# Squared-ReLU attention with a mixture of adapters: zero matmuls on PE at the start, another path for the first keys, and a new order of operations

## The chip, the cores and the metric

The kernel runs on one core of a Trainium2 chip. Its engines are PE (matrix multiplication), DVE and ACT (elementwise work, both can read the accumulators in PSUM), POOL (here it issues loads and builds two constant tiles) and SP (here it issues stores). Each engine works through its own instructions in the order in which they stand in the program, and waits on semaphores for the others. The metric is the time on the device in microseconds (us), the median of several runs; lower is better.

## The reference

Eight batches of twelve heads, with 448 positions and a head size of 64, go through an attention without softmax. The rows of its output, 768 wide, then go through eight adapters of rank 16, of which each row uses two:

```
scores = scale * np.matmul(q, k.transpose(0, 1, 3, 2))
attn = np.maximum(scores, 0.0) ** 2 / S
attn_out = np.matmul(attn, v)
...
logits = x @ w_gate                       # x: 3584 x 768
topk = np.argpartition(-logits, K, axis=1)[:, :K]     # K = 2
w = softmax over the two chosen logits
z = x[mask] @ A[e]                        # for each expert e of the row
delta[mask] += w[mask, k, None] * (z @ B[e])
return x + delta
```

Inputs and output are float32.

## The kernel before

**Tiling.** Four heads of one batch make a quad; there are 8 x 3 = 24 quads. A quad is cut into J = 7 pieces of PH = 64 keys. One piece of one quad is a step n, and there are 168 steps.

**A quad's and a step's work.** A quad's q, k and v are loaded by POOL (`load`, line 265: two DMAs for each tensor, which cast float32 to bfloat16 on the way). `tp` (line 376) transposes q and k on PE with an identity matrix (28 small transposes each, line 386), and DVE copies the result from PSUM into `qT` (line 400). Then each step has:

- `qk` (line 434): four matmuls of 64x64 by 64x448 that give scores (line 445)
- `relu` (line 456): one pass over 128x896 scores on ACT (line 465) or DVE (line 467)
- `sq` (line 475): squares for 2 or 3 steps at once, on DVE (line 483)
- `pv` (line 490): four matmuls with v (line 500), some six steps behind `qk`

After the seven steps of a quad, `xt_copy` (line 518) takes the sum from PSUM into `xt` in two copies on either ACT or DVE (line 529).

**Adapters.** 28 tiles of 128 rows. `gate` (line 538), for up to three tiles at once: logits and low-rank products on PE (line 546), a chain of small operations on DVE and ACT that picks two experts and gives their weights (lines 567 to 590), and a transpose (line 607) which is copied to `zT` (line 616). `outputs` (line 623), for one tile in two halves: the sum of x and the adapters on PE (lines 634 and 639), a copy to `osb` on ACT or DVE (line 656), and stores issued by SP (line 666). `aw_place` (line 330) brings A and w_gate into the order of the rows by matmuls with a selection matrix `sel`.

**What sets the order.** `build` (line 228) lists all operations with durations, dependences, buffers and a rank. `schedule` (line 88) is a planner that runs when the program is built: it plays the operations through with assumed durations and, on each engine, takes the available one of lowest rank (for PE with a few rules on top). The result is a fixed order for each engine and, for operations that may go to ACT or DVE, a fixed engine. Nothing of it is decided on the chip.

**The start.** `first` (line 278) treats the first quad's keys separately. The first CUT = 3 pieces come uncast by the hardware queues of SP and ACT into `raw` (line 283), and DVE casts them to `k_first` (line 298). The other four pieces come through POOL with a cast, as `k_rest` (line 294). ACT runs a warm-up activation (line 287) which loads its function table. POOL builds the identity (line 290). In `tp` the first quad has copies of its own (line 408): keys of `k_first`, queries in two halves on DVE and ACT, keys of `k_rest`. Then POOL loads in the order q1, k1, v0, q2, k2, v1, and so on (line 683 on): the v of a quad follows the q and k of the quad after it.

Of the kernel before, what the change touches and what calls it, by code (L numbers as in the profile page):

```python
# [13 lines left out]

J = 7
CUT = 3
PH = 64
QUADS = 3
NB = 8
# [7 lines left out]
PARTS = {b: ((0, S),) for b in range(NB)}  # L27

def parts(*cuts):
    x = [0, *cuts, S]
    return tuple(zip(x, x[1:]))
# [2 lines left out]
C = dict(  # L36
    tp_=2.3287, qk_=-3.679, sq_=3.7975, pv_=3.3372, xt_=-1.2131, gate_=-0.65203, id_=-0.78412,
    out_=-0.80943, zt_=6.6019, a12=(4, 7), late=6, merge_x=0, id2=2.6063, ocap=3, sqs=(2, 2, 3),
    slack=0.12309, switch=3.3127, third=4.3408, dve_relu=0.55845, relu_until=400, qk=-2.3217, sq=10,
    pv=1.0506, xt=8.4423, tp=-9.2867, tpe=4.3867, gate_mm=-4.8593, gate=-1.4524, zt=0.2432, zte=2.902,  # L40
    id=15.183, out=3.032, pace=6.5353,
)
POOLS = dict(qT=5, a1=C["a12"][0], a2=C["a12"][1], zp=2, zT=3, osb=6, w=3, q=4, k=4, v=6)

MODE_SWITCH = 0.13
HOP = 0.05
RAW = {"PE": 0.0, "ACT": 0.2, "DVE": 0.115, "POOL": 0.0, "SP": 0.0}
LAT = {"PE": 0.18, "ACT": 0.19, "DVE": 0.084, "POOL": 0.0, "SP": 0.0}
# [28 lines left out]
class Dma:  # L77


    def __init__(self, rate=0.4):  # L80
        self.rate, self.free = rate, 0.0

    def land(self, t, mb):
        self.free = max(self.free, t + 0.5) + mb / self.rate
        return self.free + 1.4


def schedule(ops, c=C):

    free = {e: 0.0 for o in ops for e in o.engs}
    avail = {e: [] for e in free}
    level = dict(POOLS, lane=4)
    freed = {b: 0.0 for b in range(c.get("nb", 8))}
    used = {"s": 0, "t": 0, "p": 0, "m": 0, "y": 0, "o": 0}
    cap = {"s": 3, "t": 1, "p": 2, "m": 2, "y": 1, "o": c.get("ocap", 1)}
    events, returns = [0.0], []
    dma = Dma()
    mode = None  # L100
    relus = []
# [13 lines left out]
    def choose(o):  # L115
        k, n = o.want
        if used[k] >= cap[k]:
            return None
        slots = sorted((x for x in range(0, c.get("nb", 8), 2) if x in freed and x + 1 in freed),
                       key=lambda x: max(freed[x], freed[x + 1]))  # L120
        if k == "s":
            if used["s"] >= 2 and any(
                x.want and x.kind != "qk" and x.ready <= t + 1e-9 and x.rank <= o.rank + c["third"]
                for x in avail["PE"]
            ):
                return None
            return [slots[0], slots[0] + 1] if slots else None
        halves = sorted((x for x in freed if x ^ 1 not in freed), key=lambda x: freed[x])
        if n == 1 and halves:
            return halves[:1]  # L130
        busy = c.get("nb", 8) // 2 - len(slots) - used["s"]
        if not slots or busy >= c.get("nb", 8) // 2 - 2:
            return None
        if n == 1 and busy == 1 and any(
            x.want and x.ready <= t + 1e-9 and x.kind in ("pv", "tp") and x.rank <= o.rank
            for x in avail["PE"]
        ):
            return None
        return [slots[0], slots[0] + 1][:n]
# [19 lines left out]
    while left:  # L159
# [9 lines left out]
        for e in free:  # L169
            if free[e] > t + 1e-9:  # L170
                continue
            o = pick(e)
            if o is None:
                continue
            st = t
            if e == "PE":
                if mode is not None and o.mode != mode:
                    st = max(t, free[e] + MODE_SWITCH)
                mode = o.mode
            o.start, o.eng = st, e  # L180
            free[e] = st + o.dur[e]
            if o.kind == "load":
                o.end = dma.land(free[e], o.mb) + (o.lat or 0.0)
            else:
                o.end = free[e] + (LAT[e] if o.lat is None else o.lat)
            for x in o.engs:
                avail[x].remove(o)
            for p in o.take:
                level[p] -= 1
            if o.want is not None:  # L190
                o.banks = choose(o)
                for x in o.banks:
                    del freed[x]
                used[o.want[0]] += 1
            back = o.end + HOP
            for p in o.give:
                returns.append((back, p))
            for owner, i in o.free:
                k = owner.want[0]
                if i is None:  # L200
                    returns.append((back, "bank", owner.banks, k, 1))
                else:
                    returns.append((back, "bank", [owner.banks[i]], k, 1 / len(owner.banks)))
            events.append(back)
            for u in o.users:
                u.missing -= 1
                near = u.engs == (e,) and o.kind != "load"
                u.ready = max(u.ready, st if u.after is o else free[e] + RAW[e] if near else back)
                if not u.missing:
                    for x in u.engs:  # L210
                        avail[x].append(u)
                    events.append(u.ready)
                    if u.kind == "relu":
                        relus.append(u)
            if o.kind == "relu":
                relus.remove(o)
            events.append(free[e])
            order.append(o)
            left -= 1
            moved = True  # L220
# [7 lines left out]
def build(k=None, c=C):  # L228
# [49 lines left out]
    def first():  # L278

        def dma(eng, g):
            eng.dma_start(out=k.raw[g * PH : g * PH + PH], in_=k.qkv[1][0, g, :, 0:2, : CUT * PH])

        def warm():
            nc.vector.memset(k.warm, 0.0)
            nc.scalar.activation(k.warm, k.warm, ACTF.Sigmoid)

        def ident():
            make_identity(nc, k.identf)  # L290

        def rest():
            for g in range(2):
                nc.gpsimd.dma_start(out=k.k_rest[g * PH : g * PH + PH],
                                    in_=k.qkv[1][0, g, :, 0:2, CUT * PH :])

        def cast():
            nc.vector.tensor_copy(k.k_first, k.raw)

        ds = [op(("SP",), 0.8, lambda: dma(nc.sync, 0), kind="load", rank=-50.0),  # L300
              op(("ACT",), 0.8, lambda: dma(nc.scalar, 1), kind="load", rank=-50.0)]
        for d in ds:
            d.mb = 2 * CUT * PH * 64 * 4e-6
        op(ACT, 1.4, warm, rank=-49.0)
        q0 = load(0, 0, 0, [])
        oi = op(("POOL",), 0.6, ident)
        ob = op(DVE, 0.2, lambda: nc.vector.tensor_copy(k.identb, k.identf), deps=[oi], rank=-60.0)
        k0 = op(DVE, dve(2 * CUT * PH, 1.92), cast, deps=ds + [ob], rank=-50.0)
        k1 = op(("POOL",), 1.17, rest, kind="load", take=("lane",), give=("lane",))
        k1.mb = 4 * (S - CUT * PH) * 64 * 4e-6  # L310
        return q0, k0, k1


# [309 lines left out]
    def outputs(tl):  # L623
# [3 lines left out]
        v = due[tl]  # L627
        W = 64 * DO
        evs, obs, prev = [], {}, None
        for h in range(2):  # L630

            def f_b(h=h):
                for x in range(3):
                    nc.tensor.matmul(  # L634
                        out=bank(obs[h])[:, x * 128 : x * 128 + 128],
                        lhsT=k.xt[:, 3 * h + x, c0 : c0 + 128], rhs=k.identb,
                        start=(x == 0), stop=False, skip_group_check=True,
                    )
                nc.tensor.matmul(  # L639
                    out=bank(obs[h])[:, :W], lhsT=T["zT", g0][:, zi], rhs=k.B[:, h * W : h * W + W],  # L640
                    start=False, stop=True, skip_group_check=True,
                )

            last = False
            if h:
                zuse[g0] -= 1
                last = zuse[g0] == 0
            prev = op(PE, 0.81, f_b, mode="128", kind="b", deps=[o_zT, b_load] + xdeps[tl], after=prev,
                      banks=("o", 1), take=() if h else ("osb",), give=("zT",) if last else (),
                      rank=v + at("id", v) + (c["id2"] if h else 0), ni=10)  # L650
            obs[h] = prev

            def ev(cp, h=h):
                if ("osb", tl) not in T:
                    new("osb", ("osb", tl), [128, 128 * DO], F32)
                cp(T["osb", tl][:, h * W : h * W + W], bank(obs[h])[:, :W])  # L656

            evs.append(evac(W, ev, deps=[prev], free=[(prev, 0)], rank=v + at("out", v)))

        def st():  # L660
            r = 0
# [18 lines left out]
        if (b, w, q) not in loaded:  # L680
            loaded[b, w, q] = load(b, w, q, [])

    for i in range(len(tiles_of) + 1):
        if i < len(tiles_of):
            loads(i, 0)
            loads(i, 1)
        if i:
            loads(i - 1, 2)
        if i == 2:
            sel_op = op(("POOL",), 1.5, sel_fn)  # L690
            a_load = op(("POOL",), 1.5, aw_fn, kind="load")
            a_load.mb = 0.4
# [4 lines left out]

    groups, t = [], 0
    while t < NT:
        m = min(3, NT - t)  # L700
        if NT - t == 4:
            m = 2
        if t == NT - 2:
# [41 lines left out]
            finish(n - c["late"] - 1)  # L745
    for n in range(NS - c["late"] - 1, NS):
        finish(n)
    return ops


@with_exitstack
def kernel(
# [31 lines left out]
    h.a_raw = const.tile([128, E, DO, R], BF16)  # L784
    h.g_raw = const.tile([128, DO, E], BF16)
    h.raw = const.tile([128, 2, CUT * PH], F32)
    h.k_first = const.tile([128, 2, CUT * PH], BF16)
    h.k_rest = const.tile([128, 2, (J - CUT) * PH], BF16)
    h.warm = const.tile([1, 8], F32)
# [39 lines left out]
```

## Time and profile before

| | us |
|---|---|
| median of 8 runs | 186.65 |
| lowest and highest | 185.52 and 187.75 |
| the profiled execution | 186.15 |
| its span, first to last instruction | 184.4 |

Busy time over the whole span, from the profile:

| engine | busy us | share |
|---|---|---|
| PE, matmuls | 168.5 | 91% |
| ACT | 161.1 | 87% |
| DVE | 159.0 | 86% |
| PE, weight loads | 99.5 | 54% |
| POOL | 90.3 | 49% |

The largest groups of instructions in it:

| line, engine, what | count | mean ns |
|---|---|---|
| 465 ACT, relu 128x896 | 162 | 952 |
| 483 DVE, squares of two steps | 48 | 1082 |
| 483 DVE, squares of three steps | 24 | 1575 |
| 529 DVE, xt copy | 42 | 618 |
| 656 ACT, output copy | 45 | 495 |
| 639 PE, half of an output | 112 | 514 |

The means of ACT and DVE include the start and end of an instruction, which overlap with its neighbours: in a row, one follows another sooner than that. Matmuls of 64x64 weights run four at a time in different parts of the array. A line of idle time such as "[0.93 <-PE ps L445]" says how long an engine stood still before the instruction and which instruction, by engine, tile and line, released it. Idle time counts only on an engine that sets the end, so the stages have to be looked at one by one.

### The profile page before, as it was taken

The numbers are of one execution on the slowest core, as the hardware profiler recorded it, in microseconds if no ns is written. First come the engines' busy times: TensorE is split into PE (matmuls) and PEld (weight loads), VectorE is DVE, ScalarE is ACT, GpSimd is POOL, SyncE is SP. The second block draws the span as 40 slices with busy tenths as digits, with TensorE's granted clock in tenths as the row PEclk, the third lists the DMA queues.
The fourth block names the chain that finished last, engine by engine and source line by source line (L and its number), as shares of the span: only waits on it lengthen the run. The fifth ranks groups of instructions, "written<-read, shape, count | busy, mean of one in ns | idle before, by whom it ended". The sixth has DMA issues, their size and how long they took to land.

```text
span 184.4 us, 7480 instructions
## 1 busy us (share of the span) xinstructions
PE 168.5 (91%) x3236; PEld 99.5 (54%) x3236; DVE 159.0 (86%) x249; ACT 161.1 (87%) x234; POOL 90.3 (49%) x155
## 2 busy tenths in 40 slices
PE   0779988889999999989999999999999999999990
PEld 0435865545555645664566455656565556556640
DVE  1499999999999999999999999999999999853600
ACT  3597899999999999999999999999999999954350
POOL 7999889898964927375735754571100000000000
PEclk9999999999999999999999999999999999999997
DMA  4999999999999999799999999999430333344775
GB/s 91 129 169 167 189 168 182 190 173 179 185 210 238 210 197 193 102 191 167 164 184 169 167 175 191 127 191 232 81 88 1 89 89 91 85 108 111 211 196 147
DMA packets 26801, 28.71 MB, mean 156 GB/s; under 512 B 4432, under 2 KB 23120, under 8 KB 26768
## 3 DMA queue, kind: packets, MB, share of 16 engines
q0 software_dynamic: 22000, 17.03, 65.9%
q1 hardware_dynamic: 4624, 11.11, 20.6%
q8 instruction: 25, 0.41, 0.9%
q10 hardware_dynamic: 144, 0.10, 0.2%
q14 instruction: 8, 0.07, 0.1%
HBM read 33.84 MB, written 11.01 MB: 243 GB/s over the span
## 4 chain that ended last, share of the span: by engine, by line
PE 56%; DVE 18%; ACT 12%; issue 5%; POOL 4%; DMA 3%; ACTq 0%; POOLq 0%
PE ps L639 17%; PE ps L445 12%; PE ps L500 12%; ACT a L465 11%; DVE a L483 9%; PE ps L634 6%; PE ps L546 4%; DVE xt L529 3%; PE ps L386 3%; DVE qT L400 3%; DMA q<-in_q_dram 3%; POOL q L271 1%; PE ps L607 1%; DVE zp L590 1%; POOL k L271 1%
## 5 line engine op out<-in xcount | busy, mean ns | idle before, releaser
L465 ACT ACTIVATE a<-ps 128x896 bf16<-128x896 f32 x162 | 139.0, 952 | 4.0 <-PE ps L445 3.7
L483 DVE TENSOR_TENSOR a<-a 128x1792 bf16<-128x1792 bf16 (+1 forms) x72 | 88.3, 1246 | 0.4 <-ACT a L465 0.4
L445 PE MATMUL ps<-qT 64*64 64x448 bf16 x672 | 62.0, 378 | 3.9 <-ACT a L465 2.3
L639 PE MATMUL ps<-B,zT 128*128 128x384 f32 x112 | 48.4, 514 | 0.0
L500 PE MATMUL ps<-a,v 64*64 64x448 bf16 x672 | 44.6, 360 | 0.7 <-DVE qT L400 0.5
L271 POOL DMA_DIRECT2D v<-in_v_dram x48 | 29.1, 623 | 28.6 <-PE ps L386 13.0
L445 PEld LDWEIGHTS <-qT 64*64 64x64 bf16 x672 | 23.6, 108 | 33.9 <-issue 24.8
L271 POOL DMA_DIRECT2D q<-in_q_dram x48 | 29.2, 627 | 6.6 <-PE ps L386 2.6
L271 POOL DMA_DIRECT2D k<-in_k_dram x46 | 28.1, 633 | 3.7 <-PE ps L445 2.4
L500 PEld LDWEIGHTS <-v 64*64 64x64 bf16 x672 | 22.6, 109 | 12.6 <-issue 4.9
L656 ACT COPY osb<-ps 128x384 f32<-128x384 f32 x45 | 22.3, 495 | 7.0 <-PE ps L639 5.9
L529 DVE CAST xt<-ps 128x448 bf16<-128x448 f32 x42 | 24.9, 618 | 3.8 <-PE ps L500 3.5
L400 DVE COPY qT<-ps 128x1792 bf16<-128x1792 bf16 x23 | 24.9, 1082 | 0.9 <-PE ps L386 0.6
L634 PE MATMUL ps<-identb,xt 128*128 128x128 bf16 x168 | 18.8, 221 | 0.1
L634 PEld LDWEIGHTS <-xt 128*128 128x128 bf16 x168 | 11.3, 97 | 13.2 <-issue 11.5
L639 PEld LDWEIGHTS ps<-B,zT 128*128 128x128 f32 x112 | 16.9, 191 | 0.0
L386 PEld LDWEIGHTS <-q 64*64 64x64 bf16 x672 | 10.9, 114 | 4.6 <-DMA q<-in_q_dram 2.0
L546 PE MATMUL ps<-awg,xt 128*128 128x136 bf16 x168 | 13.4, 224 | 0.0
L546 PEld LDWEIGHTS <-xt 128*128 128x128 bf16 x168 | 10.1, 98 | 4.8 <-issue 4.3
L386 PE MATMUL ps<-identb,q 64*64 64x64 bf16 x672 | 11.2, 199 | 0.8 <-DMA q<-in_q_dram 0.6
L386 PE MATMUL ps<-identb,k 64*64 64x64 bf16 x644 | 11.0, 199 | 0.5 <-issue 0.5
L386 PEld LDWEIGHTS <-k 64*64 64x64 bf16 x644 | 9.3, 109 | 1.7 <-DMA k<-in_k_dram 0.9
(41 smaller groups left out, 71.5 us busy)
## 6 DMA issues: line engine op xcount, KB each, us to landing
out_dram<-osb SPq DMA_DIRECT2D x56, 192.0 KB, 3.1
q<-in_q_dram POOLq DMA_DIRECT2D x48, 112.0 KB, 4.4
v<-in_v_dram POOLq DMA_DIRECT2D x48, 112.0 KB, 4.4
k<-in_k_dram POOLq DMA_DIRECT2D x46, 112.0 KB, 4.8
B<-in_moe_B_dram POOLq DMA_DIRECT2D x1, 384.0 KB, 5.3
a_raw<-in_moe_A_dram POOLq DMA_DIRECT2D x1, 192.0 KB, 4.1
k_rest<-in_k_dram POOLq DMA_DIRECT2D x2, 64.0 KB, 3.2
raw<-in_k_dram SPq DMA_DIRECT2D x1, 96.0 KB, 3.5
```

The costliest lines, as they stand in the source:

```text
L271: nc.gpsimd.dma_start(out=t[g * PH : g * PH + PH], in_=k.qkv[w][b, g, :, 2 * q : 2 * q + 2, :])
L386: nc.tensor.transpose(k.ps_b[sl * PH : sl * PH + PH, o.banks[g], (w * J + j) * PH : (w * J + j) * PH + PH], source(w, j)[r, sl], k.identb[ ...
L400: nc.vector.tensor_copy(t.rearrange("p g w x -> p g (w x)"), k.ps_b[:, m.banks[0] : m.banks[0] + 2, : 2 * S])
L445: nc.tensor.matmul(out=bank(o, sl)[g * PH : g * PH + PH, at : at + w], lhsT=t[r, g, 1, j * PH : j * PH + PH], rhs=t[r, g, 0, x0:x1], start ...
L465: nc.scalar.activation(out, flat(qk_ops[n], w), ACTF.Relu, scale=k.relu_scale)
L483: nc.vector.tensor_mul(a2, T["a1", g0], T["a1", g0])
L500: nc.tensor.matmul(out=bank(head, g)[sl * PH : sl * PH + PH, :w], lhsT=vn[r, sl, j * PH : j * PH + PH], rhs=T["a2", g0][r, i, sl * w : sl ...
L529: evac(w, lambda cp, g=g: cp(k.xt[:, g * QUADS + q, b * S + x0 : b * S + x1], bank(src, g)[:, :w]), deps=[pv_ops[n]], free=[(src, g)], ran ...
L546: nc.tensor.matmul(out=bank(zops[0])[:, t * ZW : t * ZW + ZW], lhsT=k.xt[:, do, 128 * tiles[t] : 128 * tiles[t] + 128], rhs=k.awg[:, do, : ...
L634: nc.tensor.matmul(out=bank(obs[h])[:, x * 128 : x * 128 + 128], lhsT=k.xt[:, 3 * h + x, c0 : c0 + 128], rhs=k.identb, start=(x == 0), sto ...
L639: nc.tensor.matmul(out=bank(obs[h])[:, :W], lhsT=T["zT", g0][:, zi], rhs=k.B[:, h * W : h * W + W], start=False, stop=True, skip_group_che ...
L656: cp(T["osb", tl][:, h * W : h * W + W], bank(obs[h])[:, :W])
```

## The change

Five things are edited.

1. **Zeros on PE.** A tile `zeros` is cleared by DVE, and PE multiplies it by itself SPIN = 8 times, 128x128 by 128x512, into PSUM bank 7, before the first transposes. Nothing reads the result.
2. **k_rest.** It now comes uncast by ACT's queue into `raw_rest`, in two DMAs that stand right behind that of `raw`, and DVE casts it.
3. **v one quad later.** The list of loads puts the v of a quad behind the q and k of the quad two further on.
4. **The planner's assumptions.** Engines begin at given times, PE takes twice as long until COLD = 7.0 us, and loads land by other formulas; four constants of `C` change.
5. **Ranks and engines.** RANKS shifts the ranks of some 150 operations by number, loads among them, and ENGINES fixes 16 operations to ACT or DVE.

New options (`bfull`, `merge_o`, `keep`, `gsz`) have defaults that leave the program as it was.

```diff
+SPIN = 8
...
-    slack=0.12309, switch=3.3127, third=4.3408, dve_relu=0.55845, relu_until=400, qk=-2.3217, sq=10,
+    slack=0.12338, switch=4.388, third=4.5832, dve_relu=0.20452, relu_until=400, qk=-2.3217, sq=10,
...
+RANKS = {
+    4: 25, 6: -266, 21: 137, 24: 219, 25: 204, 27: 194, 28: 242, 29: 496, 30: 237, 31: 550, 33: 638, 34:
...
+ENGINES = {
+    110: "ACT", 168: "ACT", 212: "DVE", 224: "DVE", 332: "DVE", 377: "ACT", 387: "ACT", 444: "DVE", 446:
...
+BEGIN = {"PE": 1.1, "ACT": 0.74, "DVE": 0.8, "POOL": 1.24, "SP": 0.74}
+COLD = 7.0
...
-            free[e] = st + o.dur[e]
+            free[e] = st + o.dur[e] * (2 if e == "PE" and st < COLD else 1)
...
-        def dma(eng, g):
-            eng.dma_start(out=k.raw[g * PH : g * PH + PH], in_=k.qkv[1][0, g, :, 0:2, : CUT * PH])
+        def dma(eng, t, g, j0, j1):
+            eng.dma_start(out=t[g * PH : g * PH + PH], in_=k.qkv[1][0, g, :, 0:2, j0 * PH : j1 * PH])
 
         def warm():
+            nc.scalar.activation(k.warm, k.warm, ACTF.Sigmoid)
+
+        def zeros():
             nc.vector.memset(k.warm, 0.0)
-            nc.scalar.activation(k.warm, k.warm, ACTF.Sigmoid)
+            nc.vector.memset(k.zeros, 0.0)
+
+        def spin():
+            for _ in range(SPIN):
+                nc.tensor.matmul(k.ps[:, 7, :], lhsT=k.zeros[:, :128], rhs=k.zeros, start=True, stop=True)
...
         def rest():
             for g in range(2):
-                nc.gpsimd.dma_start(out=k.k_rest[g * PH : g * PH + PH],
-                                    in_=k.qkv[1][0, g, :, 0:2, CUT * PH :])
...
+                dma(nc.scalar, k.raw_rest, g, CUT, J)
+
+        oz = op(DVE, 0.35, zeros, rank=-70.0)
+        op(PE, 0.214 * SPIN, spin, mode="128", deps=[oz], kind="spin", ni=2 * SPIN, rank=-70.0)
...
-        k1 = op(("POOL",), 1.17, rest, kind="load", take=("lane",), give=("lane",))
-        k1.mb = 4 * (S - CUT * PH) * 64 * 4e-6
+        k1 = op(DVE, dve(2 * (J - CUT) * PH, 1.92), lambda: nc.vector.tensor_copy(k.k_rest, k.raw_rest),
+                deps=[kr], rank=-30.0)
...
-    for i in range(len(tiles_of) + 1):
+    for i in range(len(tiles_of) + 2):
         if i < len(tiles_of):
             loads(i, 0)
             loads(i, 1)
-        if i:
-            loads(i - 1, 2)
-        if i == 2:
+        if i > 1:
+            loads(i - 2, 2)
+        if i == 4:
...
+    for i, d in RANKS.items():
+        ops[i].rank += d / 4
+    for i, e in ENGINES.items():
+        ops[i].engs = (e,)
```

What the planner makes of it: the work is the same but for the zeros and the cast of k_rest. Of the 168 relus DVE takes 10 (6 before), of the 48 xt copies ACT takes 21 (6 before), and of the 56 output copies DVE takes 28 (11 before). On POOL the loads begin q0, q1, k1, q2, k2, v0 (before: q0, k_rest, q1, k1, v0, q2, k2), and later loads stand in a changed order too; that of B comes seven loads later than w_gate's. On PE the transposes of k_rest stand before the first score step (before: behind it); on DVE the cast of k_rest stands before the copy of the first queries, and DVE takes the very first relu. Behind the last score step stand 17 half outputs and the gates of 7 tiles (before: 18 and 4).

## The prediction

> **What bounds the kernel now.** I read the slices first, because averages hide stages here.
>
> ```profile
> PE   0779988889999999989999999999999999999990
> ...
> DVE  1499999999999999999999999999999999853600
> ACT  3597899999999999999999999999999999954350
> ...
> PEclk9999999999999999999999999999999999999997
> ```
>
> One slice is 4.6 us. There are three stages: a ramp to about 40 us, in which ACT and DVE still stand idle at times; a plateau in which all three engines are full; and a tail from about 160 us in which only PE is. The busy time of each engine by stage gives the sizes (columns: PE, PEld, DVE, ACT, POOL, clock, DMA share, GB/s):
>
> ```profile
> 4.75:9.35 4.60, 3.75 (x104) 2.20 (x105) 2.18 (x5) 2.59 (x4) 4.60 (x9) 1.00 1.06 133
> 9.35:40.00 30.65, 26.82 (x647) 16.93 (x642) 29.45 (x39) 27.73 (x35) 28.59 (x47) 1.00 1.19 178
> ...
> 40.00:160.00 120.00, 118.51 (x2344) 68.47 (x2344) 117.68 (x176) 119.36 (x174) 53.49 (x91) 1.00 0.86 153
> 160.00:182.50 22.50, 19.37 (x149) 11.91 (x146) 9.05 (x30) 9.92 (x24) 0.00 (x0) 1.00 0.66 171
> ```
>
> On the plateau ACT is idle for 0.6 us of 120 and DVE for 2.3: **the two evacuating engines are the bound**, as most copies out of PSUM can go to either. So a microsecond that one of them loses in the ramp costs half a microsecond of span, and one that both lose costs a whole one. The tail is PE working off outputs: in the chain of waits one half output is 0.17 + 0.70 = 0.87 us.
>
> Then the timeline of the ramp shows which waits cost (start, length, engine, group, idle before it and its releaser):
>
> ```profile
> 4.34 0.36 DVE L298 CAST k_first<-raw 128x384 bf16<-128x384 f32 x1 [0.94 <-DMA raw<-in_k_dram]
> ...
> 6.04 0.39 DVE L408 COPY qT<-ps 128x448 bf16<-128x448 bf16 x1 [0.51 <-PE ps L386]
> ...
> 7.30 4.99 ACT L465 ACTIVATE a<-ps 128x896 bf16<-128x896 f32 x6 [0.68 <-PE ps L445]
> 7.52 0.42 DVE L408 COPY qT<-ps 128x512 bf16<-128x512 bf16 x1 [1.09 <-PE ps L386]
> ...
> 8.34 1.09 DVE L467 TENSOR_SCALAR a<-ps 128x896 bf16<-128x896 f32 x1 [0.39 <-PE ps L445]
> ...
> 17.92 2.74 ACT L465 ACTIVATE a<-ps 128x896 bf16<-128x896 f32 x3 [0.93 <-PE ps L445]
> ```
>
> ACT's waits after 7.30 us are 0.21 (at 12.49), 0.23 (14.45) and 0.93 (17.92), then 0.64, 0.32, 0.30 and 0.17 up to 40 us, all for scores. DVE's from 9.35 us are 0.27, 0.35, 0.32 and 0.26.
>
> Last, the groups of matmuls by shape, in the windows 8 to 18 us and 20 to 40 us:
>
> ```profile
> L445 PE MATMUL ps<-qT 64*64 64x448 bf16 x44 | 5.8, 569 | 0.8 <-DVE qT L400 0.8
> L500 PE MATMUL ps<-a,v 64*64 64x448 bf16 x25 | 3.0, 574 | 0.0
> ```
>
> ```profile
> L445 PE MATMUL ps<-qT 64*64 64x448 bf16 x88 | 9.0, 361 | 1.9 <-ACT a L465 1.6 <-issue 0.2
> L500 PE MATMUL ps<-a,v 64*64 64x448 bf16 x84 | 6.0, 352 | 0.2 <-DVE awg L345 0.2
> ```
>
> The same matmul takes 570 ns before about 18.4 us and 355 after. In the chain, 18 matmuls of weights times v fill 1.93 us at 15.56, and 20 fill 0.95 later: **half rate**. The clock row reads 9 throughout, so only the durations show it.
>
> **The change, part by part.**
>
> *Zeros on PE.* DVE's new memset follows one at 0.80 us, so PE starts at about 1.25. Half rate is about 0.38 us per four-matmul step of 448 columns (1.93 x 4/18 = 0.43 with drain), so a full-array matmul of 512 columns is about 0.43 us by estimate, and eight end at 1.25 + 3.4 = 4.7, just where k_first is cast (4.70). They delay the first transposes by 0 to 0.3 us; I take 0.1.
>
> Does it speed the clock up? The row: PE was almost gapless from 6.49 to 11.04 us (4.5 us, gaps of about 0.1) and stayed slow; it sped up at 18.4 after a gapless stretch from 13.4. By that row, 3.4 us of zeros and a few transposes do nothing. The rule is in the Trainium skill, "TensorE: Matmul & The Clock Gate", section "What's actually happening": the clock is released after a busy window of about 3.4 us, and the windows run free of the kernel's start. By it, 18.4 was a window's end, the one before ended at 15.0, and 8.2 to 11.6 failed through the 0.81 us gap at 11.04, so the trace agrees. The rule also speaks against the change: zeros exactly as long as one window seldom fill one. But if they miss, the next stretch can serve, and the clock would be up by about 10 us. By the rule ACT's waits of 0.21, 0.23 and 0.93 (1.37 us), which fall where score and value steps run at half rate, mostly go; by the row alone, none do. I take the rule, and **1.1 us of ACT**.
>
> *k_rest by ACT's queue, uncast.* POOL loses two issues of 0.61 us. ACT gains two of 0.72, so its table load moves from 1.50 to about 2.94 and its warm-up ends near 4.45; its first work is at 6.09, so 1.6 us of cover is left. DVE gains a cast of about 0.43 (the 128x512 copy took 0.42). It now stands ahead of the copy of the first queries; behind it on DVE wait that copy, the copy of the other keys and the first relu, and all score steps wait for the query copy. PE, too, transposes k_rest ahead of the first score step. By the landing times of raw (2.7 and 3.5 us from issue) the two pieces, issued at 1.46 and 2.2, land between 4.2 and 5.7; cast by 6.1 at the latest, so the copy at 6.04 slips by 0 to 0.1.
>
> Against it stands a rule, in "DMA: Bandwidth & Descriptors", "Issuing engines are not separate DMA queues": all queues share the 16 DMA engines, so another queue saves issue time only. The rows agree that the engines are full (share 1.06 from 4.75 us). Over the first 20 us SP's 96 KB took 2.3% of the engines, 0.46 us; so k_rest's 256 KB in float32 is about 1.1 us of all engines, now ahead of or among the first queries (landed by 5.46). By the issue rows the slip is 0, by the rule up to 1.1. I take 0.3, nearer the issue rows because the engines moved nothing before 2.2 us, and keep 1.1 for the range.
>
> *Order of loads.* q1 and k1 issue one slot (1.17 us) earlier, but the same bytes lie ahead of them, so I count nothing. Third queries and keys pass the first v: 13.39, the end of the longest DMA piece in the chain (5.00 us), comes about 1.2 earlier; that feeds the waits already counted. First v issues near 7.8 instead of 6.60 and lands, at 4.8 us, by 12.6; it is needed at 15.42. Later, some loads of q and k are created only 7 or 8 score steps ahead of use (30 before); at 0.9 to 1.0 us per step that covers issue and landing (1.2 + 4.4) by about 1 us. Cost nothing, 1 us for each if that is gone.
>
> *Order of operations.* DVE takes the first relu. Its waits of 1.09 and 0.39 shrink, as all keys are there early: that relu starts at about 7.0 instead of 8.34, **1.3 us of DVE**. ACT starts with the second score step, at 7.3 plus the slips above (0.1 + 0.3), less 0.2 to 0.4 if the clock is up: no change. Of ACT's 1.43 us of later waits and DVE's 1.2, I take **0.4 and 0.6** as gone, about two fifths; the ends are 0 and 2.6, since a new order may close or open waits. Work moved, by step in back-to-back runs: 4 relus to DVE, 4 x (1.01 - 0.83) = +0.7; 15 xt copies to ACT, 15 x (0.41 - 0.53) = -1.8; 7 output copies to DVE ahead of the tail, 7 x (0.48 - 0.36) = +0.8. Together -0.3, counted as nothing.
>
> *Tail.* After the last score step 17 half outputs are left instead of 18 (-0.87), but gates of 7 tiles instead of 4 (3 x 0.39 = +1.2). +0.3, set against the 0.15 of the moved work: nothing.
>
> **Sum:** (1.1 + 1.3 + 0.4 + 0.6)/2 = 1.7 us. From the profiled execution's 186.15 (span 184.4) that gives 184.45; the median of the runs is 0.5 above that execution, so for the median **184.9 us**.
>
> **Rivals.** *The shared DMA engines decide (20%), slower.* k_rest holds up the first queries by 1.1 us, its cast adds 0.4 ahead of their copy, and PE's gap after the zeros is then so long that the clock stays down. Both engines lose 1.5; only 0.4 + 0.6, halved, comes back: 186.65 + 1.5 - 0.5 = 187.65. It decides once the first relu starts after 7.8. For it: the full engines. Against: POOL's k_rest already overlapped the queries' landing.
>
> *The clock doesn't turn, and the new order replaces old waits by equal ones (20%).* Only the early relu counts: 186.65 - 0.65 = 186.0. For it: the 4.5 us stretch without effect.
>
> *The order closes nearly every wait (8%).* Ramp 1.37 + 1.43 + 1.3 + 1.2 and half of the plateau's 2.9 idle, halved: 3.4, so 183.2. Against: an order fixed beforehand meets durations that vary.
>
> **Numbers.** Forecast 52%. Runs of this kernel spread so that 0.5% (0.93 us) is about the least that can be told from no change. Faster: nearly all of the forecast, the best case and a little of the second rival, 0.60; same 0.22; slower 0.18. Range: down to all ramp and plateau waits gone, 8.2/2 = 4.1, so 182.5; up to the first rival, 187.6.
>
> **What would show it.** Matmuls of 64x448 near 355 ns before 11 us (570 up to 18 refutes the zeros); first DVE relu near 7.0 and first ACT relu by 7.4 (7.8 or later means the DMA rival); ACT's wait near 18 us gone; DVE's and ACT's idle from 9.35 to 40 us down by 2; plateau idle unchanged; the last score step 1.7 us earlier than 159.3 and the tail as long as before. More than 1.5 us of new waits for q or k after 40 us would make the forecast wrong.

## The result and the profile after

The changed kernel is slower: a median of 191.21 us (187.90 to 194.96, 20 runs) against 186.80 for the kernel before on the same chip (185.52 to 188.27, 55 runs). The ratio is **1.015, with an interval of 1.012 to 1.019**; it compares only executions within 1.5% of the fastest of their kernel, which are 6 of the 20 after and all 55 before, and so lies below the quotient of the medians, 1.024. The forecast was 184.9, with a range up to 187.6.

The profile read here is of an execution of 188.04 us with a span of 186.3. Its slices (4.66 us each):

```profile
PE   7657986789999999799699999999999999999990
...
DVE  1699997999999999999699999999999999987660
ACT  3499997999999999799699999999999999931100
```

The plateau has holes that it did not have before. In the slices at 74.5 and 88.5 us PE and ACT fall to 7 and 6, in the second of them DVE too; another hole stands at 28 us. The busy time by stage gives their size (columns: stage and its length, then PE, PEld, DVE, ACT, POOL, clock, DMA share, GB/s). First the kernel before, then the changed one:

```profile
40.00:100.00 60.00, 58.81 (x1188) 33.35 (x1188) 58.93 (x85) 59.88 (x87) 38.03 (x65) 1.00 1.07 183
```

```profile
9.35:40.00 30.65, 23.85 (x705) 15.18 (x700) 29.18 (x36) 29.29 (x40) 28.24 (x48) 1.00 1.21 180
40.00:100.00 60.00, 55.45 (x1098) 31.07 (x1097) 56.65 (x85) 56.86 (x80) 35.25 (x61) 1.00 1.01 173
```

From 40 to 100 us ACT does 3.0 us less of work and DVE 2.3 us less: (3.0 + 2.3)/2 = 2.65 us of span, by estimate. From 100 to 160 next to nothing changes (DVE 59.2 against 58.8, ACT 59.4 against 59.5). In the ramp the two engines do more than before (29.18 + 29.29 against 29.45 + 27.73), so that a part of the expected gain is there: 1.3 us of the two. The last score step starts at 161.05 us instead of 159.32, and from there to the end it is 25.2 us as against 25.1: the tail is as long as before.

PE's timeline says what the plateau waits for:

```profile
49.84 0.41 PE L422 MATMUL ps<-identb,k 64*64 64x64 bf16 x26 [0.36 <-DMA k<-in_k_dram]
...
76.48 0.22 PE L422 MATMUL ps<-identb,q 64*64 64x64 bf16 x2 [0.38 <-DMA q<-in_q_dram]
...
77.31 0.41 PE L422 MATMUL ps<-identb,q 64*64 64x64 bf16 x26 [0.62 <-DMA q<-in_q_dram]
...
90.07 0.22 PE L422 MATMUL ps<-identb,q 64*64 64x64 bf16 x2 [0.91 <-DMA q<-in_q_dram]
...
91.00 0.41 PE L422 MATMUL ps<-identb,q 64*64 64x64 bf16 x26 [0.71 <-DMA q<-in_q_dram]
```

Three loads come late: one k and two q, 2.98 us of PE in all. Before, PE's timeline shows no wait for a load between 40 and 100 us. How late they are differs from one execution to the next: in the profile of another one, of 194.46 us, PE waits 6.30 us in that stretch, for the same three. A transpose that waits holds up all of PE, which works in order; then the scores are late, and ACT, full until then, stands still (1.67 us before its relu at 91.92), and so does DVE (1.59 us before its copy at 91.76).

POOL's timeline says why the loads are late; its columns are start and length of the issues, and x6 means three loads of two DMAs:

```profile
41.30 3.56 POOL L300 DMA_DIRECT2D v<-in_v_dram  x6
44.84 1.22 POOL L300 DMA_DIRECT2D k<-in_k_dram  x2
...
68.95 1.19 POOL L300 DMA_DIRECT2D v<-in_v_dram  x2 [2.91 <-PE ps L481]
70.12 1.22 POOL L300 DMA_DIRECT2D k<-in_k_dram  x2
71.28 1.24 POOL L300 DMA_DIRECT2D q<-in_q_dram  x2
...
82.78 1.19 POOL L300 DMA_DIRECT2D v<-in_v_dram  x2 [2.14 <-PE ps L481]
83.94 1.22 POOL L300 DMA_DIRECT2D k<-in_k_dram  x2
85.11 1.24 POOL L300 DMA_DIRECT2D q<-in_q_dram  x2
```

The program's order gives their names (the number is the quad). k8, which PE wants at 49.5, stands behind v8, v18 and v6. q12 stands behind v10, which waits 2.91 us for a buffer, and k15. q14 stands behind v23, which waits 2.14 us, and k17. Steps run in order, seven to a quad, so v18 and v23 are needed more than 80 score steps later. RANKS did that: from q1 on the loads are operations 11 to 83 of the list, and the largest shifts in RANKS are theirs. A larger shift means later; v18, operation 72, has 1134 where its neighbours 71 and 73 have 2257 and 2361, and so comes far ahead of them. (The trace names a matmul of PE as what v10 and v23 waited for. That it was a free buffer is shown below, by a run with more of them.)

### The profile page after: what moved, and what is told of

Same layout as the page of the kernel before. It is cut to its first block, busy times and chain, and to the rows that moved or that the text cites. A ratio compares the mean times of both kernels' runs of the same rounds, so it can differ in the third digit from the quotient of the medians.

```text
span 192.7 us, 7488 instructions
## 1 busy us (share of the span) xinstructions
PE 170.1 (88%) x3244; PEld 98.1 (51%) x3244; DVE 166.2 (86%) x258; ACT 156.3 (81%) x227; POOL 89.6 (47%) x153
## 4 chain that ended last, share of the span: by engine, by line
PE 38%; ACT 21%; DMA 19%; POOL 12%; issue 7%; DVE 1%; ACTq 0%; POOLq 0%
ACT a L501 17%; PE ps L676 14%; DMA k<-in_k_dram 11%; PE ps L481 8%; PE ps L536 6%; DMA q<-in_q_dram 6%; PE ps L671 4%; POOL q L300 4%; POOL k L300 3%; POOL v L300 3%; PE ps L582 3%; DMA a_raw<-in_moe_A_dram 3%; PE ps L422 2%; ACT osb L708 2%; ACT xt L565 1%
## 5 line engine op out<-in xcount | busy, mean ns | idle before, releaser
L501 ACT ACTIVATE a<-ps 128x896 bf16<-128x896 f32 x158 | 135.9, 958 | 11.3 <-PE ps L481 10.5
L481 PE MATMUL ps<-qT 64*64 64x448 bf16 x672 | 60.0, 375 | 4.7 <-ACT a L501 3.3
L676 PE MATMUL ps<-B,zT 128*128 128x384 f32 x112 | 49.1, 521 | 0.0
L536 PE MATMUL ps<-a,v 64*64 64x448 bf16 x672 | 42.6, 350 | 0.7 <-ACT a L501 0.7
L481 PEld LDWEIGHTS <-qT 64*64 64x64 bf16 x672 | 22.7, 107 | 33.8 <-issue 27.7
L536 PEld LDWEIGHTS <-v 64*64 64x64 bf16 x672 | 21.2, 106 | 10.8 <-issue 3.0
L708 DVE COPY osb<-ps 128x384 f32<-128x384 f32 x28 | 15.5, 555 | 4.5 <-PE ps L676 2.9
L565 DVE CAST xt<-ps 128x448 bf16<-128x448 f32 x27 | 16.3, 617 | 0.3
L708 ACT COPY osb<-ps 128x384 f32<-128x384 f32 x28 | 14.4, 523 | 2.2 <-PE ps L676 2.1
L422 PEld LDWEIGHTS <-q 64*64 64x64 bf16 x672 | 9.7, 110 | 10.0 <-DMA q<-in_q_dram 5.8
L422 PE MATMUL ps<-identb,k 64*64 64x64 bf16 x644 | 10.8, 198 | 3.9 <-DMA k<-in_k_dram 3.8
```

Of the source, the lines that this page charges most:

```text
L422: nc.tensor.transpose(k.ps_b[sl * PH : sl * PH + PH, o.banks[g], (w * J + j) * PH : (w * J + j) * PH + PH], source(w, j)[r, sl], k.identb[ ...
L481: nc.tensor.matmul(out=bank(o, sl)[g * PH : g * PH + PH, at : at + w], lhsT=t[r, g, 1, j * PH : j * PH + PH], rhs=t[r, g, 0, x0:x1], start ...
L501: nc.scalar.activation(out, flat(qk_ops[n], w), ACTF.Relu, scale=k.relu_scale)
L536: nc.tensor.matmul(out=bank(head, g)[sl * PH : sl * PH + PH, :w], lhsT=vn[r, sl, j * PH : j * PH + PH], rhs=T["a2", g0][r, i, sl * w : sl ...
L565: evac(w, lambda cp, g=g: cp(k.xt[:, g * QUADS + q, b * S + x0 : b * S + x1], bank(src, g)[:, :w]), deps=[pv_ops[n]], free=[(src, g)], ran ...
L676: nc.tensor.matmul(out=out(h)[:, :W], lhsT=T["zT", g0][:, zi], rhs=k.B[:, h * W : h * W + W], start=False, stop=True, skip_group_check=True,)
```

## The experiments

Three theories were open. **Order of loads**: the new sequence on POOL costs all of the loss, and without it the change would do about what was forecast. **The start**: zeros and the keys by ACT's queue cost it (the first rival). **Order of compute**: the new order of all other operations costs it, without a wait for a transfer. Several runs share one edit: after the planner is done, the loads are put into another sequence, and all other operations keep their order, on every engine.

```diff
-    for o in schedule(build(h)):
+    order = schedule(build(h))
+    loads = [o for o in order if getattr(o, "key", None)]
+    loads.sort(key=lambda o: o.seq)
+    for o in reload(order, loads):
```

`reload` goes through the order and issues the next load of the wanted sequence where a load stood, as soon as its pool has a buffer free. Sorted by `seq` that is the order of the list: q0 q1 k1 q2 k2 v0 q3 k3 v1, and so on.

**The changed kernel again, and with its loads in turn.**

> The changed kernel unedited, for a profile beside the others and its spread. All theories: 188 to 195 us. Late loads (A): PE again waits some microseconds in all for q and k between 40 and 100 us, and how long differs from run to run. Late start (B): the loss is there by 20 us. Order of compute (C): the loss is spread over the plateau without any wait on a transfer.

> The changed kernel with POOL's loads of q, k and v put back in the order in which quads need them (v one quad later, as the diff's loop has it); the order on PE, DVE, ACT and SP is untouched. A (late loads): the waits for q and k after 40 us go, and with them all of the loss: 184.5 to 186 us, ratio about 0.99. B (start): a half microsecond comes back at most, ratio still 1.01 or more. C (order of compute): the same, ratio 1.01 or more.

Again: 189.82 us (4 runs), 1.013 (1.005 to 1.022). In turn: **184.63 (4 runs), 0.989 (0.983 to 0.995)**; on another chip, with 6 runs, 184.09 and 0.983 (0.979 to 0.988). These ten runs lie within 2.5 us of each other, the 24 of the changed kernel within 7.1.

> The same program as after_loads_in_turn, beside the one without zeros on the same chip: ratio 0.987 to 0.991. If zeros help, it is at least 0.2% below the one without; if they hurt, as in the kernel before, 0.2 to 0.5% above.

The order of loads is thus worth more than the whole loss, and with the start and the order of compute as they were nothing of it is left. A stage of the run in turn (columns as above):

```profile
40.00:100.00 60.00, 58.33 (x1201) 33.58 (x1201) 59.52 (x89) 59.69 (x85) 36.59 (x63) 1.00 1.05 177
```

ACT and DVE are full again from 40 to 100 us, PE waits for no load there, and the last score step starts at 156.82, 4.2 us earlier than in the changed kernel.

**The sequence alone, put into the kernel before.** The same tool gives the kernel before the changed kernel's sequence, and nothing else of the change.

```diff
+    order = schedule(build(h))
...
+    want = "q0 q1 k1 q2 k2 v0 q3 k3 v1 q4 k4 k5 k7 v2 v3 q5 v4 ... v8 v18 v6 k8 ... v10 k15 q12 ... v23 k17 q14 ..."
+    loads.sort(key=lambda o: want.index(o.key[0] + str(o.key[1])))
```

> The converse: the kernel before with the sequence of loads of the changed kernel on POOL, everything else as before. A: slower by what the changed kernel loses to late loads, 190 to 193 us, ratio 1.02 to 1.035. B and C: within 0.5% of before.

It took 194.79 us (4 runs), 1.042 (1.035 to 1.049). Two lines of PE's timeline:

```profile
87.13 0.22 PE L387 MATMUL ps<-identb,k 64*64 64x64 bf16 x2 [1.67 <-DMA k<-in_k_dram]
87.87 0.59 PE L387 MATMUL ps<-identb,k 64*64 64x64 bf16 x26 [0.52 <-DMA k<-in_k_dram]
```

ACT stands still behind them, 1.97 us before its relu at 88.93 and 1.38 before that at 91.22. PE waits 3.78 us for q and k from 40 to 100 us. So the sequence makes the waits without the other edits. It costs more here than in the changed kernel; that the other operations of the changed kernel were ordered along with it is a likely reason, not shown.

**More buffers.** Are the loads late because they stand behind others, or because far-ahead loads hold the buffers? Four more buffers for each of q, k and v, the planner unchanged:

```diff
-    h.pools = {p: ctx.enter_context(tc.tile_pool(name=f"p_{p}", bufs=POOLS[p])) for p in POOLS}
+    h.pools = {p: ctx.enter_context(tc.tile_pool(name=f"p_{p}", bufs=POOLS[p] + (4 if p in "qkv" else 0))) for p in POOLS}
```

> The changed kernel, its order of loads and all else untouched, but with four buffers more in SBUF for each of q, k and v (8, 8 and 10). If the loads come late because loads of far-off quads hold the few buffers of q and k (hoarding), POOL can now run ahead and most of the loss goes: ratio 0.985 to 1.0. If the place in POOL's queue itself is what makes them late, or the transfers are too slow, more buffers change little: ratio 1.01 or more.

> Loads in turn as in after_loads_in_turn, and the same four buffers more. Where loads in turn are never late, nothing changes: ratio 0.989 as without. If loads issued further ahead take the transfer engines from the first quads, it is worse by up to 1 us; if late loads still cost something there, better by up to 1 us.

The changed kernel with more buffers took 187.81 us (10 runs), 1.0045 (1.001 to 1.008). From 40 to 100 us, two of its transposes still wait, both for k8, and longer than in the profile without the buffers (1.94 us against 0.36):

```profile
50.81 0.22 PE L423 MATMUL ps<-identb,k 64*64 64x64 bf16 x2 [1.58 <-DMA k<-in_k_dram]
51.39 0.41 PE L423 MATMUL ps<-identb,k 64*64 64x64 bf16 x26 [0.36 <-DMA k<-in_k_dram]
```

The waits for q12 and q14 are gone, and POOL's timeline shows v10, ahead of q12, issued without a wait; v23 at 72.95 has none either:

```profile
62.12 1.27 POOL L300 DMA_DIRECT2D v<-in_v_dram  x2
```

That tells two causes apart. k8 is late for the three v issued ahead of it, which no buffer mends. q12 and q14 stand behind a v that waits for a buffer. Loads for far-off quads hold buffers too: v18 and v23 among six for v, and q15 and q17 (74 score steps ahead of use) two of the four for q. With the loads in turn more buffers bring nothing: 185.30 (18 runs), 0.992 (0.989 to 0.995).

**Three loads moved.** If that is right, moving k8, q12 and q14 is enough; with more buffers, k8 alone.

```diff
+    for x, y in (("k8", "v8"), ("q12", "v10"), ("q14", "v23")):
+        i, j = names.index(x), names.index(y)
+        names.insert(j, names.pop(i))
+        loads.insert(j, loads.pop(i))
```

> The changed kernel with three of its 71 loads moved forward on POOL: k8 (the keys of quad 8) ahead of the loads of v8, v18 and v6; q12 ahead of v10 and k15; q14 ahead of v23 and k17. All else, the other far-off loads too, stays in the changed order. If these three, by their place behind loads that wait or are not needed yet, are the loss: the waits for q and k after 40 us go, ratio 0.985 to 0.995. If the buffers that far-off loads hold are what makes q12 and q14 late: their waits stay, only that for k8 goes, ratio 1.005 to 1.012.

> Four buffers more for each of q, k and v, and k8 alone moved forward ahead of v8, v18 and v6. With more buffers the waits for q12 and q14 were gone and one for k8 was left. If the loss has just these two causes: no wait for q or k after 40 us, ratio 0.985 to 0.994. If more buffers cost time in the ramp, as loads run further ahead: 0.994 to 1.0.

Three loads: 186.04 us (22 runs), 0.994 (0.992 to 0.997). k8 with more buffers: 185.94 (10 runs), 0.993 (0.989 to 0.996). Three loads of 71, moved forward by two or three places, turn a loss of 1.3 to 1.5% into a gain of 0.6%. For q12 and q14 it is enough to stand ahead of the waiting v: they come in time with as few buffers as before, and v18, v23, q15 and q17 still hold theirs. (A wait of 0.20 us for one k, at 83.37, is all that is left there.) The run's stage from 40 to 100 us, and one line of its PE timeline:

```profile
40.00:100.00 60.00, 58.00 (x1180) 32.93 (x1176) 59.37 (x87) 59.46 (x83) 37.81 (x65) 1.00 1.06 178
```

```profile
30.64 0.41 PE L423 MATMUL ps<-identb,q 64*64 64x64 bf16 x26 [1.27 <-DMA q<-in_q_dram]
```

The plateau is mended; one late load of q or k is left ahead of it. It is q5, the sixth q, which stands behind k5, k7, v2 and v3; ACT waits 1.37 us at 31.50 in consequence. The changed kernel has the same wait (0.89 us at 29.73, the hole at 28 us in its slices), and with the loads in turn it is not there. That is the likely rest of the distance to 0.983 to 0.989, seen in traces but not tried by moving q5 alone. (PE's granted clock was 0.85 from 9.35 to 40 us in this profile, so that the length of the wait there is not compared.)

**The zeros.** On the kernel before alone, and taken out of the version with the loads in turn:

```diff
-            for _ in range(SPIN):
+            for _ in range(0):
```

> The kernel before with the zeros alone (eight matmuls of 128x512, cleared tile, ahead of the first transposes). If the zeros bring the clock up and it stays up: ACT's waits up to 18 us mostly go, 0.5 to 0.7 us less, ratio 0.996 to 0.997. If it comes up and falls back after some 3 us, as in the changed kernel's profile: 0 to 0.3 us less, ratio 0.998 to 1.0. If the zeros do nothing: ratio 1.0.

> Loads in turn, without the eight zero matmuls; the order of everything else is untouched. If the zeros carry the gain (clock up early): 1.1/2 us lost, 0.3% above loads in turn, ratio about 0.992. If the clock falls back or rises late with them anyway and the gain is the order's: within 0.2% of loads in turn, ratio 0.987 to 0.991.

> The same program as loads_in_turn_no_zeros, for more runs and a second profile. If zeros are worth nothing with loads in turn: ratio 0.987 to 0.990, as with them on the same chip.

The kernel before with zeros took 187.92 us (20 runs), 1.005 (1.003 to 1.008): slower. With the loads in turn and no zeros it is 183.97 (6 runs), 0.988 (0.985 to 0.991), and again 183.74 (6 runs), **0.981 (0.977 to 0.986)**; beside the latter, with zeros, 0.983. The zeros bring no gain that can be measured. The groups of matmuls in the kernel before with zeros (number of matmuls, busy us, mean ns of one; the four of a score step overlap, and take 0.36 to 0.38 us together at full rate), from 5 to 8 us and from 8 to 18 us, show how that comes:

```profile
L446 PE MATMUL ps<-qT 64*64 64x448 bf16 x16 | 1.5, 358 | 0.6 <-DVE qT L409 0.5
```

```profile
L446 PE MATMUL ps<-qT 64*64 64x448 bf16 x32 | 4.1, 567 | 0.8 <-DVE qT L401 0.8
```

Here the zeros do bring full rate (358 ns), from about 4.7 us. It is gone again at about 8.5 and comes back at 18.3, where the kernel before had it from 18.4. The profile of the changed kernel, from 8 to 18 us, shows another outcome; there full rate stays (the first line below). In the profile with the loads in turn, from 7 to 12.5 us, the zeros ran too and full rate is not there at all; it comes at about 13 us (the second line):

```profile
L481 PE MATMUL ps<-qT 64*64 64x448 bf16 x56 | 5.0, 361 | 1.9 <-ACT a L501 1.3 <-DVE a L503 0.6
```

```profile
L482 PE MATMUL ps<-qT 64*64 64x448 bf16 x32 | 4.4, 564 | 0.1
```

In the second profile of that program full rate comes at about 10.8 us, and without zeros at about 12.0. With the new order PE reaches full rate well ahead of the 18.4 us of the kernel before, with zeros or without.

The turns fell at different times in each execution, many of them about once or twice 3.4 us apart (8.0 and 15.0 us, 8.4 and 11.8, 14.9 and 18.5). That agrees with what the Trainium skill says in "TensorE: Matmul & The Clock Gate", "What's actually happening", of windows of 3.4 us that run free of the kernel. One or two profiles of each program can't say how often each outcome comes.

A further run filled the gaps, in which PE waits for the first queries and the last keys, with seven more zero matmuls, so that PE would be busy in the next window as well:

```diff
+                    if (b, q, w, j, g) == (0, 0, 0, 0, 1):
+                        fill(4)
...
-            m2 = op(PE, 0.13, lambda: mm(m2, 1, CUT), ...
+            m2 = op(PE, 0.13, lambda: (fill(3), mm(m2, 1, CUT)), ...
```

> Loads in turn with the eight zero matmuls and seven more in the gaps in which PE waits for the first queries (4) and for k_rest (3), so that the clock does not fall back. If an early clock that stays is worth what the prediction took (1.1 us of ACT): 0.3 to 0.5 us less than with eight zeros, ratio 0.985 to 0.987. If transfers set the ramp whatever the clock: within 0.2% of eight zeros, or up to 0.3% slower where the zeros delay the queries.

Full rate held from 5.3 to 14.9 us, and the ratio was 0.983 (0.979 to 0.988), as without. ACT's timeline from 4 to 20 us:

```profile
7.80 9.09 ACT L508 ACTIVATE a<-ps 128x896 bf16<-128x896 f32 x11 [0.64 <-PE ps L488]
...
17.82 0.92 ACT L508 ACTIVATE a<-ps 128x896 bf16<-128x896 f32 x1 [0.93 <-PE ps L488]
19.18 1.73 ACT L508 ACTIVATE a<-ps 128x896 bf16<-128x896 f32 x2 [0.44 <-PE ps L488]
```

Eleven relus in a row, and then half rate came back after 14.9 us and the waits with it, 1.37 us: they were shifted, not removed.

**k_rest by POOL again**, cast on the way, in the version with the loads in turn:

```diff
+            for g in range(2):
+                nc.gpsimd.dma_start(out=k.k_rest[g * PH : g * PH + PH], in_=k.qkv[1][0, g, :, 0:2, CUT * PH :])
...
-                dma(nc.scalar, k.raw_rest, g, CUT, J)
```

> Loads in turn, with k_rest loaded and cast by POOL behind the identity as in the kernel before, and so without DVE's cast of it; the order of everything else is untouched, so the first score step still stands behind the transposes of k_rest. If the uncast path by ACT's queue holds up the first queries on the shared transfer engines (rival of the prediction): the first relu comes earlier than 7.6 us and the time is 0.3 to 1 us less, ratio 0.984 to 0.988. If it saves POOL's slot and delays nothing: the first relu comes near 8.0, as k_rest lands at 7.06 in the kernel before, and 0.3 to 0.8 us are lost, ratio 0.991 to 0.994.

It took 185.65 us (22 runs), 0.995 (0.992 to 0.997), against 0.988 without zeros and 0.992 with more buffers on the same chip. The loads in turn alone did not run on that chip, so these two stand in for it. Its ACT timeline, and that of the version with the uncast keys, from 5 to 22 us:

```profile
7.12 0.92 ACT L504 ACTIVATE a<-ps 128x896 bf16<-128x896 f32 x1 [0.89 <-PE ps L484]
9.31 13.06 ACT L504 ACTIVATE a<-ps 128x896 bf16<-128x896 f32 x16 [1.28 <-PE ps L484]
```

```profile
8.01 0.92 ACT L502 ACTIVATE a<-ps 128x896 bf16<-128x896 f32 x1 [0.85 <-PE ps L482]
9.16 13.07 ACT L502 ACTIVATE a<-ps 128x896 bf16<-128x896 f32 x16 [0.23 <-PE ps L482]
```

The first relu comes 0.9 us earlier without the uncast keys, as the first rival had it, but ACT then waits 1.28 us and its second run starts 0.15 us later. Nothing shows the keys by ACT's queue as a loss, and they may be a gain of 0.3 to 0.7%. The smaller of these has intervals that overlap, and the loads in turn alone gave 0.983 and 0.989 on two chips, so the gain is likely, not shown.

**v one quad later, alone**, put into the kernel before as a sequence, as above, so that the planner's order of everything else stays:

```diff
+    want = """q0 q1 k1 q2 k2 v0 q3 k3  v1 q4 k4  v2 q5 k5  v3 q6 k6  v4 ... v20 q23 k23  v21 v22 v23""".split()
+    loads.sort(key=lambda o: want.index(o.key[0] + str(o.key[1])))
```

> The kernel before with v one quad later on POOL, as the diff's loop has it, and nothing else. The prediction counts its effect only with the clock's: q2 lands 1.2 us earlier than 13.39, ACT's waits of 0.21 and 0.23 shrink, 0.1 to 0.2 us of time, ratio 0.998 to 1.0. If transfers of q and k set the ramp: 0.5 us or more, ratio 0.995 to 0.997.

It took 186.21 us (21 runs), 0.995 (0.993 to 0.997). A small gain, of the size of the 0.5% that can be told.

## Why the prediction was wrong, point by point

**Order of loads: the step that failed.** It said that q and k created only 7 or 8 score steps ahead of use were covered by about 1 us, "Cost nothing, 1 us for each if that is gone". The cover was gone for three of them after 40 us, and PE paid 0.36, 1.00 and 1.62 us. The price was about right, and nought was taken in its place. What failed is the cover. In the trace of the changed kernel, PE asked for k8, q12 and q14 only 4.6, 4.8 and 4.1 us after POOL began to issue them, and began 5 score steps in that time, not 7 or 8. From the start of the issue to the end of PE's last wait for the data it was 5.0, 6.0 and 5.9 us, close to the 5.6 (1.2 + 4.4) that the prediction counted. So by its own sum these loads had less than no cover; for them the 7 or 8 steps were a miscount.

POOL's waits for buffers were no surprise to the planner, either. In the order that `schedule` makes of `build`, these three loads are issued when 44, 72 and 86 score steps are placed on PE, and in the trace 44, 73 and 86 had begun. What its plan had wrong is the landing (item 4 of the change): it reckons 4.1, 3.7 and 3.7 us from the start of the issue, where the chip took 5.0, 6.0 and 5.9. It has PE ask after 4.6, 4.9 and 4.0 us, nearly as measured. An order tuned to these formulas put the loads just where they would come in time by the formulas, and so too late on the chip.

By the runs, the sequence is worth 1.0134 - 0.9892, or 2.4% (4.5 us); with the loads in turn the time is 184.1 to 184.6, next to the 184.9 of the sum. That is in part luck, as the other terms did not come as counted (below). No rival held this mechanism; the sentence "More than 1.5 us of new waits for q or k after 40 us would make the forecast wrong" is what happened, with 2.98.

**Zeros: full rate came early in some executions, and the 1.1 us of ACT did not show in the time.** In the changed kernel's profile ACT ran 19 relus from 7.71 us without a wait, as the step had it. In other profiles full rate fell back at about 8 us, or did not come before 10.8 or 13 us. And with the loads in turn ACT ran 18 relus in a row from 9.16 us, although PE stayed at half rate to about 13 us: up to there the new order kept ACT fed, not the clock. With and without zeros the ratio is 0.983 and 0.981. The term was to be worth 0.55 us of span, 0.3%, which these intervals of half a per cent to either side can't exclude; but no run shows it. The second rival, in which the clock doesn't turn, was right in what the zeros bring and wrong in why: in some executions it does turn.

**k_rest by ACT's queue: the mechanism of the first rival, at less than its price.** The slip was larger than the 0.3 us taken; the changed kernel's timelines of DVE and of ACT:

```profile
6.27 0.66 DVE L345 CAST k_rest<-raw_rest 128x512 bf16<-128x512 f32 x1 [0.73 <-DMA raw_rest<-in_k_dram]
...
7.89 1.09 DVE L503 TENSOR_SCALAR a<-ps 128x896 bf16<-128x896 f32 x1
```

```profile
7.71 15.87 ACT L501 ACTIVATE a<-ps 128x896 bf16<-128x896 f32 x19 [0.92 <-PE ps L481]
```

The cast took 0.66 us, not 0.43 (0.43 with the loads in turn), and DVE had 0.73 us to wait for its data (1.06 with the loads in turn). The first relu on ACT starts 0.4 us later than before, 8.01 with the loads in turn (0.7 later, past the 7.8 that was to mean the rival). DVE's first relu is at 7.89: 0.45 us earlier than before, where 1.3 was counted; with the loads in turn it is at 8.39, no earlier at all. And yet the edit shows as no loss: against the version that loads these keys by POOL, what comes late on ACT at 7 us is made up by 9.3.

**Order of operations.** The ramp's terms were 3.4 us of two engines (1.1 + 1.3 + 0.4 + 0.6). ACT and DVE together were busy 60.7 us from 7.3 to 40 before, 61.9 in the changed kernel and 62.7 with the loads in turn: 1.2 and 2.1 of the 3.4. That is about 1 us of span; the rest of the gain with the loads in turn, some 1 to 2 us, is not assigned to an edit. v one quad later, counted at almost nothing, is worth 0.5% alone in the kernel before.

**Tail and plateau from 100 us on**: next to nothing, as said.

## What to carry to other kernels

A prefetch is only as early as the queue ahead of it is free, and its cover is counted from its issue to the moment at which its data is asked for, against a measured time of landing. Where loads share one in-order queue and a few rotating buffers, go through every load that stands ahead of an urgent one: those that wait for a buffer, and those needed much later, which hold buffers on top. When a search reorders prefetches by a model of their landing, compare it with plain order of need: here that was faster than the searched one by 2.4%, and three loads of 71 made most of it. Such a search spends all the slack that its model shows, so a model that lands loads 1 to 2 us too early, as here, makes them late.

## What was not expected of the hardware

Zeros cost the kernel before 0.5%. In that profile the third queries were awaited until 14.45 us instead of 13.39, though no load was moved; no run here shows why. The clock row of the kernel before reads full rate up to 18.4 us, where matmuls took 570 ns instead of 355; in the kernel before with zeros it reads 0.50 from 10 to 15 us, with matmuls as slow. So the durations of matmuls of one shape are the safer sign. The lowest time of all is that of the changed kernel with the loads in turn and no zeros: 183.74 us, 0.981 of the kernel before, which can't be told from the 0.983 with zeros.
